# Opening of a spectral filter and maxout kernel: filter loads in three parts, PSUM tiles of two banks, another order of table columns

## The chip, the cores and the metric

The kernel runs on one core of one Trainium2 chip. The metric is the device time of one execution in microseconds (us). A core has TensorE (PE in the profile, with PEld for its weight loads), VectorE (DVE), ScalarE (ACT), GpSimd (POOL) and SyncE (SP), and 16 DMA engines that all queues share. The results of matmuls go to PSUM, which has eight banks of 2 KB on each of 128 partitions; VectorE and ScalarE empty them here, and GpSimd reads SBUF only. About 0.2% (1 us) is what a measurement of this kernel can tell from no change.

## The reference

The input x has 8 sequences of 3072 tokens of 256 channels. Each channel is filtered along the sequence in the frequency domain, and the result goes through a two-branch maxout layer:

```python
X = np.fft.rfft(x, axis=1)
Y = X * (filt_r + 1j * filt_i)[None]
y = np.fft.irfft(Y, n=3072, axis=1)            # 8 x 3072 x 256
g = np.maximum(y @ w1, y @ w2)                 # 24576 x 1024
out = g @ w_out                                # 24576 x 256
```

## The kernel before

**The transform as matmuls.** 3072 = 96 x 32. For a sequence, a first step multiplies by a cosine and sine table of size 96 (C1), a second one by a table of size 32 with the twiddle factors (U, one 64-column block for each of 24 values u), then comes the product with the filter, and the two steps go back (VP and VQ, then G1). A visit is a sixth of the frequencies; the index v (or n) counts six visits, each of two values w, and w, g gives u = 2w + g. The second step s2 (L371) leaves a pair of PSUM tiles px, s = 0 and 1, and the product of each with the filter (L380) gives a tile pq for the step back.

**The filter.** F (128 partitions) holds the filter in the order that px has. load_f (L109) fills partitions 0 to 31 and 64 to 95: 16 partitions with frequencies in rising order (L117), 16 with falling order (L120), and one more small load for the frequency at the fold (L124). These loads cast from float32 and go through GpSimd's queue. double_f (L128) copies each group of 32 partitions to the next 32, by VectorE (L130) or by SP's DMA (L132). The filter comes in two parts, WP: visits 0 to 3 (w 0 to 7), doubled by VectorE, and visits 4 and 5 (w 8 to 11), doubled by four DMAs on SP's queue. On that queue the four loads of the layer's weights (WS, L279) stand behind them.

**The opening, batch 0.** It is written out by hand from L562 on, and each engine runs its instructions in the order in which they are written. Tables are computed on VectorE and ScalarE (table_c, tables_u, sines_u). s1t (L495) does the first step for the eight tiles of x, each with two PSUM tiles pa, which ScalarE (for the last tiles VectorE too) writes to at2; spin (L556) fills TensorE with matmuls that compute nothing. t1 (L507) transposes at2 in six groups, one PSUM bank each, emptied by VectorE and ScalarE in turn to bt. table_v and put_v (L252, L267) make VP and VQ out of U, in two halves (h) and two kinds (q), with two banks and two or three evictions each; the factor one half of frequency zero is the scale hv in L272. s2 and the products of the six visits follow. For the visits in POOLED, ScalarE copies px of s = 1 to SBUF (stage_x, L591), and GpSimd multiplies it there; visit 5's is shared half and half by VectorE and GpSimd (L386). s3t (L518) does the step back of a visit into two PSUM banks pt, which ScalarE, and for visits 4 and 5 VectorE too, writes to zT. The visits go in the order 1, 0, 2, 3, 4, 5.

GpSimd's queue is, in order: eight loads of x, small tables, 18 filter loads, a load of x of batch 1, its products, two loads of x, half of Wd (L290), the load of Wo (L287), a load of x, the other half of Wd.

**The stream after it.** From L646 on, t2 brings zT to zr, s4 does the last step to y, and a loop over 64 token tiles does the layer: moe_h (L442; Wd = w1 - w2, a rectified product) and moe_o (L463), which adds y @ M, with M = w2 @ w_out. A list with planned steps places the work of the next batches in between: s1, visits (s2, products, s3, through DRAM with zd), z_read. The PSUM pools ps (six banks) and pso (two banks) serve the opening and the stream alike.

Of the kernel before, what the change touches and what calls it, by code (L numbers as in the profile page):

```python
# [11 lines left out]
OP = mybir.AluOpType  # L12
# [14 lines left out]
def kernel(  # L27
# [40 lines left out]
    ps = ctx.enter_context(tc.tile_pool(name="ps", bufs=6, space=bass.MemoryType.PSUM))  # L68
    pso = ctx.enter_context(tc.tile_pool(name="pso", bufs=2, space=bass.MemoryType.PSUM))
# [3 lines left out]
    pq0 = setup.enter_context(tc.tile_pool(name="pq0", bufs=6))  # L73
    ctx.enter_context(tc.manual_schedule())
# [33 lines left out]
    WP = ((0, 8), (8, 12))  # L108

    def load_f(h):  # L110
        w0, w1 = WP[h]
        n = 2 * (w1 - w0)
        for g in range(2):
            for ri, f in enumerate((filt_r, filt_i)):
                k0 = 24 * g + 2 * w0
                src = bass.AP(f.tensor, f.offset + k0 * D, [[96 * D, 16], [D, n], [1, D]])
                G.dma_start(out=F[64 * g:64 * g + 16, ri, w0:w1].rearrange("p w s d -> p (w s) d"), in_=src)  # L117
                n0 = 1 if k0 == 0 else 0
                src = bass.AP(f.tensor, f.offset + (96 - k0 - n0) * D, [[96 * D, 16], [-D, n - n0], [1, D]])
                G.dma_start(out=F[64 * g + 16:64 * g + 32, ri, w0:w1].rearrange("p w s d -> p (w s) d")[:, n0:n],  # L120
                            in_=src)
                if n0:
                    src = bass.AP(f.tensor, f.offset + 48 * D, [[96 * D, 16], [1, D]])
                    G.dma_start(out=F[16:32, ri, 0, 0], in_=src)  # L124
# [17 lines left out]

    V.memset(W1, 1.0)
# [3 lines left out]
    kc = init.tile([NP, NW, 2, 2], FP32)  # L147
    kap = init.tile([128, NW, 2], FP32)
# [3 lines left out]
    hv = init.tile([128, 2, 1], FP32)  # L152
    load_x(0, 0, 1)
    G.iota(pid, pattern=[[1, 1]], base=0, channel_multiplier=1, allow_small_or_imprecise_dtypes=True)
    G.iota(kc, pattern=[[2, NW], [24, 2], [1, 2]], base=0, channel_multiplier=0,
           allow_small_or_imprecise_dtypes=True)
    load_x(0, 1, 1)
    G.iota(kap, pattern=[[2, NW], [24, 2]], base=0, channel_multiplier=0,
# [4 lines left out]
    for c in range(3, 8):  # L163
        load_x(0, c, 1)
    for q in range(2):
        G.memset(hv[:, q], 1.0)
        for r in (0, 32):
            G.memset(hv[r:r + 1, q], 0.5 * (1 - q))
    load_f(0)
    load_f(1)  # L170
# [3 lines left out]
    def table_c():  # L174
# [4 lines left out]
        kf = kc.rearrange("p w g s -> p (w g s)")  # L179
# [16 lines left out]
    def tables_u():  # L196
# [24 lines left out]
        V.tensor_scalar(t1[:, 0], kap.rearrange("p w g -> p (w g)"), a_, base, OP.mult, OP.add)  # L221
# [19 lines left out]
    def sines_u(h):  # L241
        uv = ua.rearrange("p u c s j -> p u (c s j)")
        S.activation(U[:, NW * h:NW * h + NW], uv[:, NW * h:NW * h + NW], AF.Sin, bias=zero, scale=TWO_PI)

    def table_g():
        pg = ps.tile([96, NP], FP32, tag="ps", name="pg")
        TE.matmul(pg, C1, I128[0:NP, 0:NP], start=True, stop=True)
        S.activation(G1, pg, AF.Copy)

    def table_v(h, q):  # L250
        pool, tag = (pso, "po") if h else (ps, "ps")
        pv = [pool.tile([128, 6, 64], FP32, tag=tag, name="pv%d" % s) for s in range(2)]  # L252
        for i in range(6):
            for g in range(2):
                for s in range(2):
                    rows = slice(64 * s, 64 * s + 64)
                    u = 2 * (6 * h + i) + g
                    if q == 0:
                        TE.matmul(pv[s][64 * g:64 * g + 64, i], U[rows, u], I128[rows, rows], start=True, stop=True)
                    else:  # L260
                        TE.matmul(pv[s][64 * g:64 * g + 32, i], U[rows, u, 32:64], I128[rows, rows],
                                  start=True, stop=True)
                        TE.matmul(pv[s][64 * g + 32:64 * g + 64, i], U[rows, u, 0:32], NI[rows, rows],
# [3 lines left out]
    def put_v(h, q, pv):  # L267
        for s in range(2):
            i0 = 1 if h == 0 and s == 0 else 0
            tab = VQ if q else VP  # L270
            if i0:
                S.activation(tab[:, 0, 0], pv[0][:, 0], AF.Identity, bias=zero, scale=hv[:, q])  # L272
            S.activation(tab[:, 6 * h + i0:6 * h + 6, s], pv[s][:, i0:6], AF.Copy)  # L273
# [97 lines left out]
    def s2(b, v):  # L371
        px = [ps.tile([128, 2, D], FP32, tag="ps", name="px%d" % s) for s in range(2)]
        for i in range(2):
            for s, g in ((0, 0), (1, 1), (0, 1), (1, 0)):
                u = 2 * (2 * v + i) + g
# [4 lines left out]
    def product(E, v, s, px, pool=None):  # L380
# [3 lines left out]
        return pq  # L384

    def shared_product(v, s, px, xs_, pool):  # L386
        pq = pool.tile([128, 2, 2, D], BF16, tag="pq", name="pq")
        V.tensor_tensor(pq[:, 0], px, F[:, 0, 2 * v:2 * v + 2, s], OP.mult)
        G.tensor_tensor(pq[:, 1], xs_, F[:, 1, 2 * v:2 * v + 2, s], OP.mult)
        return pq  # L390

    def s3(b, v, pq):
# [9 lines left out]
        for g in range(2):  # L402
            S.activation(zt[:, :, g], pz[g], AF.Copy)  # L403
        nc.sync.dma_start(out=zd[b][4 * v:4 * v + 4].rearrange("u p d -> p u d"),
                          in_=zt.rearrange("p i g d -> p (i g) d"))
# [89 lines left out]
    def s1t(c):  # L495
        for dc in range(2):
            pa = ps.tile([128, 4, 96], FP32, tag="ps", name="pa")
            for m in range(4):
                TE.matmul(pa[:, m], xb[0, c][:, m, 128 * dc:128 * dc + 128], C1, start=True, stop=True)
            o_ = at2[:, dc].rearrange("p u q m -> p (u q) m")[:, :, 4 * c:4 * c + 4]  # L500
            i_ = pa.rearrange("p m q -> p q m")
            if dc == 1 and c >= 6:
                V.tensor_copy(o_, i_)
            else:
                S.activation(o_, i_, AF.Copy)

    def t1(n, engine):  # L507
        pb = ps.tile([128, 4, D], BF16, tag="ps", name="pb")
        for i in range(4):
            for dc in range(2):  # L510
                TE.transpose(pb[:, i, 128 * dc:128 * dc + 128],
                             at2[:, dc, 4 * n + i].rearrange("p q m -> p (q m)"), I128)
        if engine is S:
# [226 lines left out]
```

## Time and profile before

| | us |
|---|---|
| three runs | 503.47, 503.74, 504.51; median 503.74 |
| profiled execution | 503.8 |
| its span | 502.0 |
| TensorE busy | 488.4 (97%) |
| VectorE busy | 331.9 (66%) |
| ScalarE busy | 308.3 (61%) |
| GpSimd busy | 257.5 (51%) |

The profile is of one execution. Its views, which are quoted below, are: the page with the busy share of each engine in 40 slices of the span; windows, one line for each stretch, with the busy time of each engine in it and the count of its instructions, then the clock that was granted to TensorE (1.00 is full), the DMA engines' share and GB/s; the chain, which follows the work that ended last back from the end; and the instructions of an engine in order of time, each with its start, its length, the line of the kernel, the tile written and the tiles read, how many were merged into the row, and in brackets the idle time before it and what ended that. A DMA's row on a queue is the time of its issue; the time from issue to landing is given separately. L12 is line 12 of the kernel before.

### The profile page before, as it was taken

The numbers are of one execution on the slowest core, as the hardware profiler recorded it, in microseconds if no ns is written. First come the engines' busy times: TensorE is split into PE (matmuls) and PEld (weight loads), VectorE is DVE, ScalarE is ACT, GpSimd is POOL, SyncE is SP. The second block draws the span as 40 slices with busy tenths as digits, with TensorE's granted clock in tenths as the row PEclk, the third lists the DMA queues.
The fourth block names the chain that finished last, engine by engine and source line by source line (L and its number), as shares of the span: only waits on it lengthen the run. The fifth ranks groups of instructions, "written<-read, shape, count | busy, mean of one in ns | idle before, by whom it ended". The sixth has DMA issues, their size and how long they took to land.

```text
span 502.0 us, 13079 instructions
## 1 busy us (share of the span) xinstructions
PE 488.4 (97%) x5299; PEld 362.1 (72%) x5303; DVE 331.9 (66%) x518; ACT 308.3 (61%) x629; POOL 257.5 (51%) x338
## 2 busy tenths in 40 slices
PE   8688999999999999999999999999999999999997
PEld 3455777777777777777777777777777777777775
DVE  7876688457865777457765687557765687555553
ACT  6776478647774676557764586647774465544442
POOL 7893569547463864645654855537632221222220
PEclk9989999999999999999999999999999999999999
DMA  7999789995799667986779558896769235411112
GB/s 125 150 252 217 230 229 290 306 274 171 212 268 260 175 204 234 250 229 189 198 244 275 187 177 245 235 239 197 197 181 255 78 111 153 168 65 64 64 64 84
DMA packets 77966, 97.20 MB, mean 194 GB/s; under 512 B 8017, under 2 KB 54354, under 8 KB 77842
## 3 DMA queue, kind: packets, MB, share of 16 engines
q1 hardware_dynamic: 64642, 66.73, 49.6%
q0 software_dynamic: 13264, 29.64, 20.3%
q8 instruction: 41, 0.67, 0.6%
q14 instruction: 19, 0.16, 0.1%
HBM read 53.87 MB, written 47.19 MB: 201 GB/s over the span
## 4 chain that ended last, share of the span: by engine, by line
PE 90%; DMA 5%; POOL 2%; issue 1%; ACT 1%; DVE 0%; SPq 0%; POOLq 0%; DVEq 0%
PE po L476 34%; PE ph L448 33%; PE po L474 8%; PE pz L399 5%; PE py L428 4%; PE pa L349 2%; DMA F<-in_filt_r_dram 2%; PE px L376 2%; DMA Wo<-in_moe_w_out_dram 2%; POOL xb L88 1%; DMA F<-F 1%; PE pr L549 1%; POOL pq L382 0%; PE pt L528 0%; PE pm__1132 L306 0%
## 5 line engine op out<-in xcount | busy, mean ns | idle before, releaser
L476 PE MATMUL po<-Wo,gt 128*128 128x256 bf16 x1536 | 261.0, 273 | 0.2 <-DMA Wo<-in_moe_w_out_dram 0.2
L452 ACT ACTIVATE gt<-ph 128x384 bf16<-128x384 f32 x321 | 157.0, 496 | 147.9 <-PE ph L448 147.3
L461 POOL DMA_DIRECT2D out_dram<-ot x186 | 102.6, 555 | 187.1 <-DVE ot L488 184.4
L476 PEld LDWEIGHTS <-gt 128*128 128x128 bf16 x1536 | 146.6, 98 | 66.1 <-issue 10.3
L450 DVE TENSOR_SCALAR gt<-ph 128x384 bf16<-128x384 f32 x191 | 104.9, 552 | 63.1 <-PE ph L448 59.9
L382 DVE TENSOR_TENSOR pq<-px,F 128x1024 bf16<-128x1024 f32 x91 | 107.0, 1219 | 24.2 <-PE px L376 22.6
L448 PEld LDWEIGHTS <-Wd 128*128 128x128 bf16 x1024 | 96.5, 98 | 12.9 <-POOL Wd L292 1.4
L103 POOL TENSOR_TENSOR xb<-XF 128x512 bf16<-128x512 f32 x48 | 61.2, 1276 | 41.3 <-DMA XF<-in_x_dram 21.2
L488 DVE COPY ot<-po 128x512 f32<-128x512 f32 x95 | 65.1, 685 | 25.3 <-PE po L476 25.0
L104 POOL TENSOR_TENSOR xb<-XF 128x512 bf16<-128x512 f32 x48 | 61.0, 1271 | 0.0
L403 ACT ACTIVATE zt<-pz 128x512 bf16<-128x512 f32 x84 | 45.6, 595 | 11.5 <-PE pz L399 8.4
L353 ACT ACTIVATE at<-pa 128x512 bf16<-128x512 f32 x96 | 51.8, 610 | 1.2 <-PE pa L349 0.8
L428 PE MATMUL py<-G,zr 96*128 96x96 bf16 x512 | 32.7, 206 | 0.2
L428 PEld LDWEIGHTS <-zr 96*128 96x128 bf16 x512 | 29.0, 97 | 2.5 <-DVE zr L552 0.4
L399 PE MATMUL pz<-pq,VP 64*64 64x256 bf16 x336 | 21.9, 281 | 0.0
L376 PE MATMUL px<-bt,U 64*64 64x256 bf16 x384 | 19.8, 278 | 1.2 <-ACT VQ L273 0.7
L399 PE MATMUL pz<-pq,VQ 64*64 64x256 bf16 x336 | 20.9, 269 | 0.0
L349 PE MATMUL pa<-xb,CT 64*64 64x512 bf16 x192 | 19.5, 383 | 0.0
L399 PEld LDWEIGHTS <-VP 64*64 64x64 bf16 x336 | 9.7, 105 | 13.3 <-issue 13.3
L376 PEld LDWEIGHTS <-U 64*64 64x64 bf16 x384 | 10.4, 109 | 3.9 <-issue 3.3
L559 PE MATMUL pd<-W 128*128 128x512 bf16 x30 | 10.5, 462 | 1.7 <-DVE zero L145 1.5
L552 DVE COPY zr<-pr 96x1024 bf16<-96x1024 bf16 (+1 forms) x8 | 5.2, 649 | 8.0 <-PE pr L549 8.0
(429 smaller groups left out, 609.7 us busy)
## 6 DMA issues: line engine op xcount, KB each, us to landing
out_dram<-ot POOLq DMA_DIRECT2D x186, 128.0 KB, 3.3
XF<-in_x_dram SPq DMA_DIRECT2D x96, 192.0 KB, 4.6
ad<-at SPq DMA_DIRECT2D x56, 192.0 KB, 3.3
bt<-ad SPq DMA_DIRECT2D x14, 768.0 KB, 9.1
zd<-zt SPq DMA_DIRECT2D x42, 256.0 KB, 2.7
zr<-zd SPq DMA_DIRECT2D x56, 192.0 KB, 4.8
WS<-in_moe_w_dram SPq DMA_DIRECT2D x4, 512.0 KB, 5.1
xb<-in_x_dram POOLq DMA_DIRECT2D x8, 192.0 KB, 5.8
```

Source lines behind the costliest of these rows:

```text
L103: G.tensor_tensor(t_[:, 0], f[:, 0], f[:, 1], OP.add)
L104: G.tensor_tensor(t_[:, 1], f[:, 0], f[:, 1], OP.subtract)
L353: S.activation(at[:, m0:m0 + 2], pa[g], AF.Copy)
L382: E.tensor_tensor(pq, px.rearrange("p (o i) d -> p o i d", o=1).to_broadcast([128, 2, 2, D]), F[:, :, 2 * v:2 * v + 2, s], OP.mult)
L399: TE.matmul(pz[g][64 * s:64 * s + 64, i], tab[64 * g:64 * g + 64, 2 * v + i, s], pq[s][64 * g:64 * g + 64, q, i], start=(q == 0), stop=(q ...
L428: TE.matmul(py[:, m], zr[b][:, 4 * i + m, 128 * dc:128 * dc + 128], G1, start=True, stop=True)
L448: TE.matmul(ph, Wd[:, dc, 128 * j:128 * j + 128], y_[:, dc], start=(dc == 0), stop=(dc == 1))
L450: V.tensor_scalar(gt[tt][:, j], ph, 0.0, None, OP.max)
L452: S.activation(gt[tt][:, j], ph, AF.Relu)
L461: E.dma_start(out=dst, in_=ot[tt // 2][:, 3 * (tt % 2) + c])
L476: TE.matmul(p_, g_[:, n - 2, blk], Wo[:, n - 2], start=(e == 0), stop=(e == 9))
L488: V.tensor_copy(ot[tt // 2][:, e - 1:e + 1], po[0])
```

## The change

- **Filter in three parts.** WP is (0, 4), (4, 8), (8, 12). Only the first (visits 0 and 1) is doubled by VectorE; the second and third by SP's DMAs. The filter loads are 26.
- **Alternating partitions.** The rising and the falling frequencies stand on even and odd partitions of each group of 32, not on two blocks of 16. The columns of U, and so the rows of VP and VQ, follow: (c j s) for (c s j), and u = 4v + 2g + i for 2(2v + i) + g, also in the later batches.
- **Pairs of banks in the opening.** A pool named pair holds four tiles of two banks each, and every PSUM tile of the opening comes from it, the spin matmuls' too; ps and pso are made when it is given back. s1t, put_v and s3t empty a pair with one ScalarE instruction (s1t of the last tile and s3t of visit 5 with one of ScalarE and one of VectorE); t1 works on two groups at a time, one emptied by VectorE and one by ScalarE.
- **The factor one half** is put on a copy U0 of U's first block by one VectorE instruction, so put_v needs no eviction of its own for it.
- **Order of the opening.** sines_u(1) is written ahead of put_v; VectorE's doubling goes r before i; the visits go 0 to 5, with s3t right behind each visit's products for 0 to 3. POOLED is (2, 4, 5) for (0, 2, 3, 4), and visit 5 is no longer shared.

```diff
-    WP = ((0, 8), (8, 12))
+    WP = ((0, 4), (4, 8), (8, 12))
...
-                G.dma_start(out=F[64 * g:64 * g + 16, ri, w0:w1].rearrange("p w s d -> p (w s) d"), in_=src)
+                G.dma_start(out=F[64 * g:64 * g + 32:2, ri, w0:w1].rearrange("p w s d -> p (w s) d"), in_=src)
...
+    def two(name):
+        return pair.tile([128, 2, 512], FP32, tag="pair", name=name)
...
+    U0 = init.tile([128, 2, 64], BF16)
...
+    G.memset(hv, 1.0)
     for q in range(2):
-        G.memset(hv[:, q], 1.0)
-        for r in (0, 32):
-            G.memset(hv[r:r + 1, q], 0.5 * (1 - q))
-    load_f(0)
-    load_f(1)
+        G.memset(hv[0:64, q, 0:64:32], 0.5 * (1 - q))
+    for h in range(3):
+        load_f(h)
...
+        if h == 0:
+            V.tensor_tensor(U0, U[:, 0:1].to_broadcast([128, 2, 64]), hv, OP.mult)
...
     def put_v(h, q, pv):
-        for s in range(2):
-            i0 = 1 if h == 0 and s == 0 else 0
-            tab = VQ if q else VP
-            if i0:
-                S.activation(tab[:, 0, 0], pv[0][:, 0], AF.Identity, bias=zero, scale=hv[:, q])
-            S.activation(tab[:, 6 * h + i0:6 * h + 6, s], pv[s][:, i0:6], AF.Copy)
+        S.activation((VQ if q else VP)[:, 6 * h:6 * h + 6].rearrange("p i s m -> p s i m"), pv, AF.Copy)
...
     def s1t(c):
+        pa = two("pa")[:, :, 0:384].rearrange("p c (m q) -> p c m q", m=4)
...
+        if c < 7:
+            S.activation(o_, i_, AF.Copy)
         else:
-            V.tensor_copy(bt[0][:, 4 * n:4 * n + 4], pb)
+            S.activation(o_[:, 0], i_[:, 0], AF.Copy)
+            V.tensor_copy(o_[:, 1], i_[:, 1])
+
+    def t1(n):
+        pb = pair.tile([128, 2, 4, D], BF16, tag="pair", name="pb")
...
     def s3t(v, pq):
...
+        pz = two("pz").rearrange("p g (i s r c m) -> p g i s r c m", i=2, s=2, r=2, c=2)
...
+        if v < 5:
+            S.activation(zv, i_, AF.Copy)
+        else:
+            S.activation(zv[:, 0:2], i_[:, 0:2], AF.Copy)
+            V.tensor_copy(zv[:, 2:4], i_[:, 2:4])
...
-    for g in range(2):
-        for ri in range(2):
-            double_f(1, g, ri, nc.sync)
+    for h in (1, 2):
+        for g in range(2):
+            for ri in range(2):
+                double_f(h, g, ri, nc.sync)
...
-    for n in range(6):
-        t1(n, S if n % 2 else V)
-    put_v(0, 0, table_v(0, 0))
-    for g in range(2):
-        for ri in range(2):
+    for n in (0, 2, 4):
+        t1(n)
+    sines_u(1)
+    for ri in range(2):
+        for g in range(2):
             double_f(0, g, ri, V)
...
-    POOLED = (0, 2, 3, 4)
+    POOLED = (2, 4, 5)
...
-    pxs = {v: s2(0, v) for v in (1, 0)}
-    stage_x(0)
+    pxs = {v: s2(0, v) for v in (0, 1)}
+    put_v(0, 0, table_v(0, 0))
     put_v(0, 1, table_v(0, 1))
     pxs[2] = s2(0, 2)
     stage_x(2)
-    sines_u(1)
     put_v(1, 0, table_v(1, 0))
+    put_v(1, 1, table_v(1, 1))
     pxs[3] = s2(0, 3)
-    stage_x(3)
-    put_v(1, 1, table_v(1, 1))
-    for v in (1, 0, 2):
+    for v in range(4):
         pqs[v] = products(v)
-    s3t(1, pqs[1])
-    pxs[4] = s2(0, 4)
-    stage_x(4)
-    pqs[3] = products(3)
-    s3t(0, pqs[0])
-    pxs[5] = s2(0, 5)
-    stage_x(5)
-    for v in (2, 3):
         s3t(v, pqs[v])
+        if v < 2:
+            pxs[v + 4] = s2(0, v + 4)
+            stage_x(v + 4)
```

## The prediction

> **What bounds the kernel now.** I read the page first, then the stretches of the opening, then the chain that ended last, then each engine's instructions in order of time between 14 and 38 us.
>
> ```profile
> span 502.0 us, 13079 instructions
> PE   8688999999999999999999999999999999999997
> ```
>
> Each digit is 12.55 us. TensorE is full from the fifth digit on; only the first four have room, and every function whose work differs after the change and is not a mere renumbering runs there. Busy time of the engines (PE, PEld, DVE, ACT, POOL), granted clock, DMA share:
>
> ```profile
> 20.00:25.00 5.00, 2.47 (x111) 1.57 (x118) 4.47 (x5) 4.01 (x9) 4.93 (x5) 0.77 0.70 117
> 25.00:30.00 5.00, 4.53 (x128) 2.81 (x121) 4.57 (x5) 3.22 (x7) 5.00 (x3) 0.54 0.94 213
> 50.00:55.00 5.00, 5.00 (x44) 3.68 (x43) 3.86 (x8) 3.03 (x6) 0.00 (x0) 1.00 0.73 200
> ```
>
> From 50 us TensorE has no gap, so what the opening gains or loses goes to the end whole. The chain, in order of time (start, length):
>
> ```profile
> 16.69 4.13 DMA F<-in_filt_r_dram
> ...
> 21.61 3.23 DMA F<-F
> ...
> 30.64 2.10 POOL pq L382
> 32.73 1.15 POOL pq L389
> ...
> 37.19 9.41 DMA Wo<-in_moe_w_out_dram
> ```
>
> It runs over the filter's last part: load, copy into the second half of the partitions by SP's DMA, POOL's products of visits 4 and 5, then POOL's queue (two loads of x, Wd, Wo). Those engines one by one:
>
> ```profile
> 16.22 0.48 POOL L117 DMA_DIRECT2D F<-in_filt_r_dram  x1
> 16.69 0.54 POOL L120 DMA_DIRECT2D F<-in_filt_r_dram  x1
> ...
> 18.22 1.25 POOL L117 DMA_DIRECT2D F<-in_filt_r_dram  x1
> 19.57 1.49 POOL L120 DMA_DIRECT2D F<-in_filt_r_dram  x1
> 21.05 1.24 POOL L117 DMA_DIRECT2D F<-in_filt_i_dram  x1
> 22.28 1.17 POOL L120 DMA_DIRECT2D F<-in_filt_i_dram  x1
> ...
> 24.02 6.31 POOL L382 TENSOR_TENSOR pq<-xs,F 128x1024 bf16<-128x1024 f32 x3
> ```
> ```profile
> 18.15 1.22 DVE L130 COPY F<-F 32x4096 bf16<-32x4096 bf16 x1
> ...
> 19.72 3.60 DVE L130 COPY F<-F 32x4096 bf16<-32x4096 bf16 x3
> 23.82 5.75 DVE L382 TENSOR_TENSOR pq<-px,F 128x1024 bf16<-128x1024 f32 x5 [0.50 <-DVE F L130]
> 30.60 2.36 DVE L382 TENSOR_TENSOR pq<-px,F 128x1024 bf16<-128x1024 f32 x2 [1.03 <-DMA F<-F]
> ```
> ```profile
> 27.33 0.67 PE L376 MATMUL px<-bt,U 64*64 64x256 bf16 x8
> 27.44 1.09 ACT L538 ACTIVATE zT<-pt 128x512 bf16<-128x512 f32 x2 [1.07 <-PE pt L528]
> ```
>
> Three things are to be seen. A filter load costs POOL about 0.5 us to issue, 64 KB or 128 KB alike, but 1.17 to 1.49 us while VectorE's copies L130 run. VectorE then waits for SP's last copy until 30.60, and POOL takes up visit 4 at 30.63, so 30.5 is when the last copy landed. And TensorE computes the next px at 27.33 while ScalarE is only beginning to empty the pt before it: there is PSUM to spare.
>
> **The change, part by part.** The sum is made against the profiled execution, 503.8 us with a span of 502.0 (0.06 above the median of 503.74).
>
> *Loads of the filter, POOL's queue.* Eighteen loads become 26: eight more issues at 0.50 (start to start at 16.22, 16.69, 17.22, 17.69, 18.22) are +4.0 us. The ninth to sixteenth load of POOL's queue each starts just after a landing of the x load eight places earlier (9.92 after x3, 14.11 after x7, whose matmul starts at 13.88), so eight are in flight at most; that order stays. After the change the eighth filter load still goes at 14.11 and the other 18 follow. The ones after x7 start about 0.5 us earlier, since the 64 KB loads ahead land sooner (before, two waited until 14.88 and 15.66). VectorE's copies halve: 4 of 1.22 become 4 of about 0.65 (half, plus a little fixed cost). Four issues during the long copies took 5.15 us for 2.0, a loss of 3.1 in 4.9 us of copying; in proportion 2.6 us of copies cost 1.6, and if each issue just ends with the next copy, 0.4. I take 1.1, a relief of 2.0. Last issue: 22.28 + 4.0 - 0.5 - 2.0 = 23.8. Its landing took 4.1 with an issue of 1.17; with an issue of 0.53 it is 3.4, so 27.2 in place of 26.4. Bounds: 26.5 (no loss to copies) and 28.5.
> [...]
>
> *Copies on SP's queue.* Four of 128 KB become eight: visits 2 and 3 (part two) now come by DMA too. In the trace such a copy took 2.9, 3.2, 5.4 and 4.0 us from issue to landing. All are queued ahead of the four loads of WS, which move later with the last of them (27.01 before) by about 1; WS for Wd's first half landed at 32.7, over 2 us ahead of its use at 34.90. Last copy, with the last row's 4.0: 27.2 + 4.0 = 31.2 in place of 30.4. Bounds 29.4 (26.5 + 2.9) and 33.4 (28.0 + 5.4).
>
> *Products.* POOL's list (0, 2, 3, 4 and half of 5: 4 x 2.13 + 1.16 = 9.7 us) becomes (2, 4, 5): 6.4 us. But both 4 and 5 need the last copy, and behind it POOL now has 2 x 2.13 = 4.3 where it had 2.13 + 1.16. So POOL is through at 31.2 + 0.1 + 4.3 = 35.6 in place of 33.89: +1.7. VectorE does nine products instead of seven and a half, 10.9 for 9.2 us, but its copies are 2.3 shorter: it starts near 21.6, has done four by 26.3, waits for part two's copies (load issued about 20, landed 23.6, copied 27), and does 2 and 3 by 30.6 and the last two by 33.7. It is off the path.
>
> *PSUM pairs.* Eight banks are now four pairs. Program order alone says which pair each tile can get. While px0, px1 and px2 are alive, pv(1,0), pv(1,1) and px3 follow each other through one pair; px4 can only have pz0's pair, px5 only pz1's, after ScalarE has emptied them. These are new waits on TensorE's queue. What stands behind them there are the s3t matmuls, and behind those ScalarE's evictions. Durations: an eviction of 384 took 0.49, of 512 0.60; so 768 is 0.82 and 1024 is 1.0 (a 1024 row at 43.33 took 1.02), beside 0.87 and 1.09 for two single ones. Merging saves ScalarE about 0.05 each time. In order: t1 starts some 0.2 later (one eviction of 768 instead of two engines in x tile 6), ScalarE is through with bt at 19.1, the sines 0.93, 20.0; two put_v 21.65; xs2 22.25; put_v 23.1; then pv(1,1) on TensorE 0.75 with its hand-overs, put_v 24.7; px3 25.5; s3t(0) with its filler 1.6 at the granted clock of 0.54, 27.2; eviction 28.3; px4 29.0; s3t(1) 30.6; eviction 31.7; px5 32.3. From here 0.85 each on TensorE and 1.0 on ScalarE: evictions end at 34.3, 35.3 and 36.3, and the last half at 37.0, where the last one before ended at 35.07: +1.9. Bounds: +0.7, if TensorE is warm in s3t(0) and s3t(1) (0.9 for 1.6 twice), and +2.5.
>
> *Cheap or free.* The half-scale on U0 is one small VectorE instruction near 13, in a gap (VectorE waits 0.59 at 14.43). The six memsets of hv become three, 0.3 us ahead of the first load, given back at the wait on x3. The sines move from 22.40 to 19.1, taking away TensorE's 1.5 us wait for U; what is late next there is the pair of pv(1,1), costed above. The new order of rows in U, F, zt and the tables changes no size of any instruction from 50 us on: nothing, hidden or not.
>
> *Sum.* POOL's path +1.7 and ScalarE's +1.9 run side by side and meet in s3t(5) and Wd; the later sets it. Behind them the order is untouched: f1, t2, s4, the first moe_h need zT and Wd, and Wo is issued 3.3 us after POOL's products and landed 9.4 later, so all move by about 1.9. 503.8 + 1.9 = 505.7.
>
> **The rivals.**
> - *B, the last copy is slow.* The eight copies share the engines with x of batch 1 (384 KB, issued before at 23.43, landed at 28.7), as the third copy before did with 5.4 us. With the late bound T = 33.4 POOL ends at 37.8, +3.9: 507.7. For it: the DMA share of 0.94 at 25 to 30 us, and 0.5 MB more copies; against: only one copy of four took that long.
> - *C, no change.* Filter loads move at x's pace. x tiles of 192 KB came about 1.0 us apart, 190 KB per us; the first seven filter loads, 540 KB, landed from 13.9 to 17.6, 145 KB per us. On alternating partitions, with short latencies (26.5 + 2.9 = 29.4), POOL ends at 33.8, -0.1; a warm TensorE must then bring ScalarE's path to +0.7 or less: 503.7 to 504.5, I take 504.2. Against: in the second half the loads are spaced by their issue, not by their bytes. [...]
> - *D, faster.* POOL's 3.3 us of less work comes through, because POOL and not the filter was the limit: it ran from 24.02 to 30.33 without a break and met visit 4 at 30.63. Place: the last SP copy; it decides if that lands by 28.1, when POOL would leave v2 (26.0 + 2.1). POOL then ends at 32.4, -1.5: 502.3. Against: with the shortest latencies seen (3.4 and 2.9) the last load would have to be issued at 21.8, 17 issues in 7.1 us, 0.42 each, where the trace has 0.47 to 0.57.
>
> **How the numbers follow.** A, the forecast, 505.7: 0.55, own range +1.0 to +3.0. B 0.14, C 0.18, D 0.13. A measurement can tell about 0.2%, 1.0 us. D is faster, C the same, A and B slower, less 0.01 of A's low edge: 0.13, 0.19, 0.68. The range reaches over C and most of B, 502.9 to 508.0; D and B's upper edge, together under 0.2, lie outside.
>
> **What would show it.** Right: 26 filter loads, the last issued near 23.8; the last F<-F landing near 31; VectorE's products from about 21.6, with a wait for F<-F before visit 2; POOL idle before visit 4, its products ending near 35.6; TensorE waiting for zT evictions before px4 and px5 and for VQ before px3; Wo landing near 48.5 instead of 46.6; the stretches beyond 60 us unchanged. Wrong: POOL busy without a gap from its first product, or a last copy before 29, or px4 computed while pz0 is still full.

## The result and the profile after

The changed kernel takes 512.25 us (median of six runs, 511.18 to 513.96) against 503.75 (six runs, 503.42 to 504.51): a ratio of 1.017, with a 95% interval of 1.0149 to 1.0191. It is 8.5 us slower, where 1.9 were forecast; the range ended at 508.0. Its profiled execution took 512.8 us, the span is 511.0, 9.0 more than before.

The page of the changed kernel, the span and the slices (12.8 us each) of TensorE and of its clock:

```profile
span 511.0 us, 13076 instructions
PE   7677999999999999999999999999999999999996
PEclk9857999999999999999999999999999999999999
```

The loss is in the first four slices, as forecast: three of them hold less than before (8, 6, 8, 8 became 7, 6, 7, 7), and in the third the granted clock is 0.5. Stretches of the changed kernel (busy us of PE, PEld, DVE, ACT, POOL, then clock, DMA share, GB/s):

```profile
20.00:25.00 5.00, 2.35 (x139) 1.96 (x139) 4.76 (x7) 4.64 (x6) 5.00 (x10) 0.74 1.01 187
25.00:30.00 5.00, 3.55 (x89) 1.78 (x65) 5.00 (x5) 2.32 (x3) 2.44 (x2) 0.50 0.99 176
30.00:35.00 5.00, 3.89 (x84) 2.48 (x84) 1.28 (x2) 2.26 (x3) 0.00 (x0) 0.50 0.88 273
35.00:40.00 5.00, 2.56 (x81) 1.79 (x78) 2.36 (x2) 2.44 (x3) 4.45 (x3) 0.84 0.68 230
40.00:45.00 5.00, 3.59 (x42) 2.51 (x38) 1.11 (x2) 1.78 (x3) 4.97 (x6) 0.50 0.84 143
60.00:65.00 5.00, 5.00 (x48) 3.82 (x47) 3.89 (x7) 2.33 (x6) 1.35 (x3) 1.00 0.73 227
```

Three things differ from before. The DMA engines are full from 20 to 30 us (shares of 1.01 and 0.99, where they were 0.70 and 0.94). GpSimd does nothing at all between 30 and 35 us. And TensorE runs at half its clock for most of 25 to 45 us (0.50 granted in three of the four stretches, 0.84 in the other), where before it had 1.00 in every stretch from 30 us on.

The chain of the changed kernel that ended last, in order of time (start, length):

```profile
24.25 5.23 DMA F<-in_filt_i_dram
29.54 5.59 DMA F<-F
...
35.55 1.89 POOL pq L388
...
37.64 2.14 POOL pq L388
...
39.82 0.84 PE pz L526 x24
40.68 0.61 ACT zT L534
41.31 0.70 DVE zT L535
...
43.07 0.85 PE pr L546 x8
...
46.06 0.61 PE ph L448 x2
```

It is the chain of the forecast: the last load, the last copy, GpSimd's two products, the last s3t, then the step to the layer. GpSimd in order of time, changed kernel:

```profile
24.25 0.54 POOL L119 DMA_DIRECT2D F<-in_filt_i_dram  x1
24.78 0.52 POOL L87 DMA_DIRECT2D xb<-in_x_dram  x1
27.14 2.14 POOL L388 TENSOR_TENSOR pq<-xs,F 128x1024 bf16<-128x1024 f32 x1 [1.84 <-DMA F<-F]
35.55 4.21 POOL L388 TENSOR_TENSOR pq<-xs,F 128x1024 bf16<-128x1024 f32 x2 [6.28 <-ACT zT L532]
```

It stands idle for 6.28 us ahead of visit 4. The row names an eviction of ScalarE as what ended the wait, but what held it was the copy, which landed at 35.13: VectorE begins its last two products at 35.55 too, and in the kernel with single banks below both begin at 34.7, where the row names the copy. In both kernels the start comes 0.42 us after the landing (34.29 there). ScalarE's evictions of zT, changed kernel:

```profile
28.43 1.02 ACT L532 ACTIVATE zT<-pz 128x1024 bf16<-128x1024 f32 x1 [2.24 <-PE pz L526]
31.09 1.02 ACT L532 ACTIVATE zT<-pz 128x1024 bf16<-128x1024 f32 x1 [1.16 <-PE pz L526]
34.36 1.02 ACT L532 ACTIVATE zT<-pz 128x1024 bf16<-128x1024 f32 x1 [0.91 <-PE pz L526]
35.87 1.02 ACT L532 ACTIVATE zT<-pz 128x1024 bf16<-128x1024 f32 x1 [0.48 <-PE pz L526]
38.30 1.02 ACT L532 ACTIVATE zT<-pz 128x1024 bf16<-128x1024 f32 x1 [1.41 <-PE pz L526]
40.68 0.60 ACT L534 ACTIVATE zT<-pz 128x512 bf16<-128x512 f32 x1 [1.35 <-PE pz L526]
```

The moments side by side (us; "first ph" and "first po" are the first matmuls of the layer):

| | before | forecast | after |
|---|---|---|---|
| last filter load issued | 22.28 | 23.8 | 24.25 |
| landed | 26.4 | 27.2 | 29.48 |
| last copy F<-F landed | 30.5 | 31.2 | 35.13 |
| GpSimd's products through | 33.89 | 35.6 | 39.76 |
| zT complete | 35.19 | 37.0 | 42.0 |
| first ph | 37.48 | 39.4 | 46.06 |
| Wo landed | 46.6 | 48.5 | 50.8 |
| first po | 46.64 | 48.5 | 54.67 |

Of the 9.0 us, 5.9 are there when GpSimd is through, and 2.7 more come between that and the first ph.

### The profile page after: what moved, and what is told of

It is laid out like the page before. It is cut to its first block, busy times and chain, and to the rows that moved or that the text cites. A ratio compares the mean times of both kernels' runs of the same rounds, so it can differ in the third digit from the quotient of the medians.

```text
span 511.0 us, 13076 instructions
## 1 busy us (share of the span) xinstructions
PE 490.9 (96%) x5300; PEld 364.6 (71%) x5302; DVE 331.0 (65%) x518; ACT 307.7 (60%) x611; POOL 255.7 (50%) x341
## 4 chain that ended last, share of the span: by engine, by line
PE 82%; DMA 9%; POOL 4%; DVE 2%; issue 1%; ACT 1%; SPq 0%; POOLq 0%; ACTq 0%
PE po L476 31%; PE ph L448 29%; PE po L474 8%; PE pz L399 5%; PE py L428 4%; PE pa L351 2%; PE px L382 2%; DMA xb<-in_x_dram 2%; DMA zd<-zt 1%; DMA bt<-ad 1%; DMA XF<-in_x_dram 1%; DMA out_dram<-ot 1%; DMA F<-F 1%; DMA F<-in_filt_i_dram 1%; POOL F L116 1%
## 5 line engine op out<-in xcount | busy, mean ns | idle before, releaser
L388 DVE TENSOR_TENSOR pq<-px,F 128x1024 bf16<-128x1024 f32 x93 | 109.3, 1219 | 27.7 <-PE px L382 23.3
L382 PE MATMUL px<-bt,U 64*64 64x256 bf16 x384 | 19.7, 283 | 3.6 <-ACT VP L275 1.1
L382 PEld LDWEIGHTS <-U 64*64 64x64 bf16 x384 | 10.4, 109 | 6.2 <-issue 4.9
```

What stands on the lines that cost most here:

```text
L388: E.tensor_tensor(pq, px.rearrange("p (o i) d -> p o i d", o=1).to_broadcast([128, 2, 2, D]), F[:, :, 2 * v:2 * v + 2, s], OP.mult)
```

## The experiments

Ratios stand to the kernel before on the same chip, with 95% intervals. Where a diff starts from the changed kernel, it stands against 1.017.

### One part of the change alone, or undone

**Three parts alone** (the kernel before, with the filter's parts and the copies of the changed one):

```diff
-    WP = ((0, 8), (8, 12))
+    WP = ((0, 4), (4, 8), (8, 12))
...
-    load_f(0)
-    load_f(1)
+    for h in range(3):
+        load_f(h)
...
-    for g in range(2):
-        for ri in range(2):
-            double_f(1, g, ri, nc.sync)
+    for h in (1, 2):
+        for g in range(2):
+            for ri in range(2):
+                double_f(h, g, ri, nc.sync)
```

> The kernel before with the filter in three parts alone: 26 loads, eight F<-F copies on SP's queue, VectorE doubles only visits 0 and 1; blocks of 16 partitions, single banks, its own order and its own POOLED. Theory 'congestion': the last copy lands near 34 to 35 instead of 30.4, and of the two products behind it POOL has one and a half; the time rises by 3.5 to 5 on 504.3, to about 508.5. Theory 'pairs': the filter's parts cost nothing where the banks are single, the time stays within 1 of 504.3.

Measured: 509.38 us, ratio 1.0097 (1.0069 to 1.0126), 5.2 us more. Its chain:

```profile
25.12 3.19 DMA F<-in_filt_i_dram
28.36 6.00 DMA F<-F
35.12 2.13 POOL pq L382
...
43.14 0.59 PE ph L448 x2
```

The last copy takes 6.00 us and lands at 34.4, 3.9 later than before; GpSimd idles 2.60 us and is through at 38.36. So the three parts cost some 5 us with all of PSUM as it was. Of the 3.9 us, 2.8 are the later issue of the last load (25.12 for 22.28) and 2.0 the longer copy (6.00 for 4.03), while its landing is 0.9 shorter (3.19 for 4.11).

**Alternating partitions alone** (the kernel before):

```diff
-                G.dma_start(out=F[64 * g:64 * g + 16, ri, w0:w1]...
+                G.dma_start(out=F[64 * g:64 * g + 32:2, ri, w0:w1]...
...
-                G.dma_start(out=F[64 * g + 16:64 * g + 32, ri, w0:w1]...
+                G.dma_start(out=F[64 * g + 1:64 * g + 32:2, ri, w0:w1]...
...
-        S.activation(U[:, NW * h:NW * h + NW], uv[:, NW * h:NW * h + NW], AF.Sin, bias=zero, scale=TWO_PI)
+        us = slice(NW * h, NW * h + NW)
+        S.activation(U[:, us].rearrange("p u (c j s) -> p (u c) s j", c=2, s=2),
+                     uv[:, us].rearrange("p u (c s j) -> p (u c) s j", c=2, s=2), AF.Sin, bias=zero, scale=TWO_PI)
```

> The kernel before with the alternating partitions alone (F's rows, U's columns). Loads and copies keep their number and size. All theories but one expect no change, 503.8 to 504.8. [...]

Measured: 503.65 us (ten runs), ratio 0.9985 (0.9972 to 0.9997). At most a slight gain; no cost. The theory that the spread over partitions matters, which the next run's expectation states, is the one that looked for a change here. It is the fastest kernel of the study, by less than the 0.2% that were called the bound of a difference.

**Blocks of 16 partitions put back** (the changed kernel; the diff above the other way round).

> The changed kernel with the filter's signs and the columns of U back on two blocks of 16 partitions; all else as changed. Theory 'partitions' (the new spread over partitions slows the loads or the copies): the last F<-F copy lands at 32 or earlier instead of 35.1, and the time falls from 512.3 to about 508. Theory 'congestion' (too many copies and loads share the DMA engines between 20 and 35 us) and theory 'pairs' (waits for whole PSUM pairs) both expect no gain: 512 to 513, with loads that land a little later, since 16 neighbouring partitions take a load no faster.

Measured: 511.58 us, ratio 1.0137 (1.0114 to 1.016). Nearly all of the loss stays. Alternation is not its cause.

**Second part doubled by VectorE too** (the changed kernel, three parts, four copies on SP's queue):

```diff
-    for h in (1, 2):
-        for g in range(2):
-            for ri in range(2):
-                double_f(h, g, ri, nc.sync)
+    for g in range(2):
+        for ri in range(2):
+            double_f(2, g, ri, nc.sync)
...
+    for ri in range(2):
+        for g in range(2):
+            double_f(1, g, ri, V)
```

> The changed kernel with the second part of the filter doubled by VectorE too, so SP's queue has four F<-F copies instead of eight; loads, order and pairs stay. Theory 'congestion': without half a megabyte of copies the last load lands near 27.5 instead of 29.5 and the last copy near 31.5 instead of 35.1; POOL's products end near 36 instead of 39.8 and the time falls by 3 to 4, to about 508.5. Theory 'pairs': ScalarE's evictions and TensorE are held by each other and not by the copies, the time falls by 1 at most, to 511.3 or more.

Measured: 507.81 us, ratio 1.0075 (1.0054 to 1.0095). The 26 loads are all still there, and GpSimd in this kernel is through at 36.45, 3.3 earlier:

```profile
32.23 4.22 POOL L388 TENSOR_TENSOR pq<-xs,F 128x1024 bf16<-128x1024 f32 x2 [4.87 <-DMA F<-F]
```

So the four added copies are a cause: without them 3.5 us of loss stay out of 8.5. What the eight added loads cost by themselves is not shown. The ratio is that of two parts (next), but GpSimd waits for the last copy until 32.23 here, while there it takes up visit 4 at 30.43 with no wait for a copy of F. The pairs can hide this difference: in both kernels ScalarE evicts visits 2 to 4 without a gap, and zT is complete at 38.6.

**Two parts** (the changed kernel):

```diff
-    WP = ((0, 4), (4, 8), (8, 12))
+    WP = ((0, 8), (8, 12))
...
-    for h in range(3):
+    for h in range(2):
         load_f(h)
...
-    for h in (1, 2):
+    for h in (1,):
```

> The changed kernel with the filter in two parts as before: 18 loads, VectorE doubles visits 0 to 3, four F<-F copies; partitions, order and pairs as changed. Theory 'congestion': the last copy lands at 30.4 as in the kernel before, POOL's products end at 30.5 + 4.3 = 34.8, the time falls by about 5, to 507.3; what is left over 503.75 is POOL's longer tail and the pairs. Theory 'pairs': still 510 or more, since ScalarE empties the last pair near 40.

Measured: 507.88 us, ratio 1.0072 (1.0057 to 1.0087). With the parts undone 3.6 us of loss stay. The last filter load is issued at 20.20 and the last copy by 25.25; GpSimd, through at 35.51, now waits for ScalarE's copies of px (3.87 and 0.83 us, ahead of visits 4 and 5), not for the filter. ScalarE's evictions of visits 2 to 4, with the second part doubled by VectorE (above):

```profile
34.27 3.09 ACT L532 ACTIVATE zT<-pz 128x1024 bf16<-128x1024 f32 x3 [0.76 <-PE pz L526]
```

and with two parts:

```profile
34.05 3.09 ACT L532 ACTIVATE zT<-pz 128x1024 bf16<-128x1024 f32 x3 [0.75 <-PE pz L526]
```

That the pairs are the second cause is shown by the single banks below.

**Single banks** (the changed kernel, three parts; each tile of two banks becomes two tiles of one, and each merged eviction two):

```diff
-    pair = setup.enter_context(tc.tile_pool(name="pair", bufs=4, space=bass.MemoryType.PSUM))
+    pair = setup.enter_context(tc.tile_pool(name="pair", bufs=8, space=bass.MemoryType.PSUM))
...
-        return pair.tile([128, 2, 512], FP32, tag="pair", name=name)
+        return [pair.tile([128, 512], FP32, tag="pair", name="%s%d" % (name, k)) for k in range(2)]
...
-        S.activation((VQ if q else VP)[:, 6 * h:6 * h + 6].rearrange("p i s m -> p s i m"), pv, AF.Copy)
+        for s in range(2):
+            S.activation((VQ if q else VP)[:, 6 * h:6 * h + 6, s], pv[s], AF.Copy)
```

> The changed kernel with every PSUM tile of the opening in banks of its own (eight of one bank, two evictions for two banks), same order of work, same filter path. Theory 'pairs': without waits for whole pairs VectorE and ScalarE empty bt at the same time (bt done near 19 instead of 20.8), the last zT eviction is no longer behind ScalarE's (0.7), the time falls by 3 or more, to 509 or less. Theory 'congestion': POOL still ends its products near 39.5, since the last copy lands at 35; only the 0.7 at the end and some of the 1.4 us at the start of t1 come back where they count, and the time is 511 to 512.

Measured: 511.14 us, ratio 1.0135 (1.012 to 1.015): 6.8 us of the 8.5 stay. GpSimd in this kernel:

```profile
34.71 4.20 POOL L388 TENSOR_TENSOR pq<-xs,F 128x1024 bf16<-128x1024 f32 x2 [4.77 <-DMA F<-F]
```

The pairs are gone, ScalarE is done with bt at 18.93 instead of 20.84, and the fourth eviction of zT starts at 32.36 for 35.87; but everything then waits for the copy, only 0.8 us earlier than in the changed kernel. While the copy is late, the pairs are mostly hidden behind it.

**Two parts and single banks** (both diffs above on the changed kernel).

> The changed kernel with the filter in two parts and every PSUM tile of the opening in single banks. Two parts alone came to 507.9. Theory 'pairs': what is left comes from waits for whole pairs and from px4 and px5 behind evictions that now end bank by bank: VectorE's products start 0.7 to 0.9 earlier, zT is done near 37 instead of 38.6, the time is 506 to 506.5. If the order of the visits and POOLED are what is left (VectorE's nine products end near 34), it stays above 507.

Measured: 504.11 us (ten runs), ratio 1.0005 (0.9995 to 1.0015). The whole loss is gone. Alternation, U0, the order of visits and the new division of the products are still in this kernel and, taken together, cost nothing that can be measured. Three parts alone +5.2 and the pairs with two parts +3.6 make 8.8, near the 8.5 measured for both, but the two do not simply add up: beside three parts, single banks took off only 1.7 of the 8.5, and in single banks three parts leave 6.8.

### Why the last copy is late

**x of batch 1 out of the copies' way** (the changed kernel; the load is issued after GpSimd's products instead of after the last filter load):

```diff
     load_fn()
-    load_x(1, 0, 2)
...
-    for c in (2, 4):
+    for c in (0, 2, 4):
         load_x(1, c, 2)
```

> The changed kernel with the load of batch 1's first x tiles (384 KB as written, 768 KB read) issued behind POOL's products, not ahead of them. Theory 'congestion' in the form that any bytes count: F's last copies have the DMA engines more to themselves between 25 and 32 us, the last lands near 33.5 instead of 35.1, POOL is through 1.5 us earlier; f1(1, 0) then waits for this load (issued near 38, landed near 43), which is needed at 42; the time is 511 to 512.5. If only the number of loads and copies counts (each waits for the one before it), the last copy stays at 35 and the time rises, to 513.

Measured: 509.94 us, ratio 1.011 (1.0083 to 1.0138). Its chain:

```profile
23.91 3.71 DMA F<-in_filt_i_dram
27.67 2.78 DMA F<-F
30.87 3.00 POOL pq L387 x2
...
35.02 4.92 DMA xb<-in_x_dram
...
43.27 0.64 PE ph L447 x2
```

With eight copies and 26 loads as in the changed kernel, but without the 384 KB of x, the last load takes 3.71 us for 5.23 and the last copy 2.78 for 5.59: it lands at 30.45, 4.7 us earlier. What held the copies was the engines' time that this load took: the DMA share from 25 to 30 us is 0.74 without it, 0.99 with it. GpSimd's products end at 35.09. Only part of this reaches the end, since the first step of batch 1 now waits for its x, which lands at 39.9, and the first ph comes at 43.06.

**Three parts with x in the middle** (three parts alone; x of batch 1 behind GpSimd's third product):

```diff
-    load_x(1, 0, 2)
...
+    load_x(1, 0, 2)
     for v in (4, 5):
         pqs[v] = products(v)
```

> The kernel before with the filter in three parts, as in b1_threeparts, and with the load of batch 1's first x tiles (384 KB) issued by POOL behind its products of visits 0, 2 and 3 instead of ahead of them. In b1 that load was in flight together with the last F<-F copies, which took 6 us each, and the last landed at 34.4. Theory 'congestion by that load': the last copy takes 3 to 4 and lands by 31, POOL's products end near 34.5 instead of 38.4, zT near 36, and the time is 504.5 to 505.5 instead of 509.4. Rival 'too many copies': the eight copies hold each other, the last still lands near 34, the time stays above 508.

Measured: 511.08 us, ratio 1.0139 (1.012 to 1.0158), no faster than the three parts alone and rather slower. GpSimd is through at 35.9 for 38.36, so the copy is early again; but the load of x, issued at 32.07 beside the 2 MB of WS, takes 8.47 us, TensorE waits 3.5 us for it, and the first ph comes at 44.66 for 43.12. In each of these kernels something in the stretch took longer: the last copy in the changed one (5.59 us, 2.78 with x moved), x here (8.47, 5.35 before), the loads of WS in the next (a median of 8.7, 5.1 before).

**Single banks, x behind visit 2's product, and fillers** (the changed kernel, three parts; the single banks above, the fillers of the next experiment, and):

```diff
-    load_x(1, 0, 2)
...
         s3t(v, pqs[v])
+        if v == 2:
+            load_x(1, 0, 2)
```

> The changed kernel with three things undone or added at once: the load of batch 1's first x tiles issued by POOL behind its product of visit 2, single banks, and the fillers of e8_warm. If the three causes (that load's contention with the copies, waits for whole pairs, the cold clock) make up the loss, the last copy lands near 30.7, POOL's products end at 35.1, zT near 36.3 with a warm TensorE, and the time is 504.5 to 506. If something else of the change costs time, it stays above 507.

Measured: 509.16 us (507.23 to 510.87), ratio 1.01 (1.0064 to 1.0137), above the range that was expected. The last copy lands near 31.5 and GpSimd is through at 36.1, but it then waits 0.47 us for WS, which was pushed later and took 8.7 us, and the first ph comes at 40.13, 2.7 later than before. In none of the three places tried for x are the eight copies free.

### The low clock behind the last product

**Fillers in s3t** (the changed kernel; three to five matmuls that compute nothing, instead of one, at the head of the last four s3t):

```diff
-        TE.matmul(pz[:, 0].rearrange("p i s r c m -> p (i s r c m)"), W1[:, 0:128], W1, start=True, stop=True)
+        for _ in range({2: 3, 3: 3, 4: 4, 5: 5}.get(v, 1)):
+            TE.matmul(pz[:, 0].rearrange("p i s r c m -> p (i s r c m)"), W1[:, 0:128], W1, start=True, stop=True)
```

> The changed kernel with more filler matmuls ahead of s3t of visits 2 to 5 (3, 3, 4 and 5 instead of 1 each), which TensorE computes while it would wait for products; nothing else. Theory 'cold clock': with the granted clock at 1.00 from 38 us on instead of 0.50 between 40 and 45, the way from the last product (39.8) to the first ph (46.1) shrinks from 6.3 to about 4.4, and the time from 512.3 to about 510.5. If Wd and Wo hold the first matmuls of the layer anyway, no gain, 512 to 513; if the fillers stand in the way of s3t they cost up to 1.

Measured: 509.98 us, ratio 1.0118 (1.01 to 1.0135), 2.3 us less than the changed kernel. The stretches of this kernel:

```profile
40.00:50.00 10.00, 8.09 (x89) 4.92 (x83) 6.45 (x13) 5.89 (x12) 7.63 (x9) 1.00 0.97 144
...
30.00:40.00 10.00, 8.03 (x149) 4.04 (x147) 3.24 (x3) 4.69 (x5) 4.45 (x3) 0.74 0.77 247
```

and of the changed kernel:

```profile
40.00:50.00 10.00, 8.29 (x74) 5.36 (x71) 4.75 (x10) 4.57 (x9) 7.54 (x9) 0.69 0.99 149
...
30.00:40.00 10.00, 6.45 (x156) 4.28 (x158) 3.63 (x4) 4.69 (x5) 4.45 (x3) 0.67 0.78 252
```

GpSimd is through at the same 39.8 in both. With the fillers TensorE is busy for 8.03 us for 6.45 in the ten before 40 us, is granted a clock of 1.00 for 0.69 in the ten after it, and does the first ph at 44.33 for 46.06. So 1.7 of the 2.7 us between the last product and the first ph are the clock by these traces, and 2.3 by the times of the two kernels.

**The same fillers with two parts** (the two parts above).

> The changed kernel with the filter in two parts (507.88, 1.0072) and the fillers in s3t(2) to s3t(5) that took 2.3 us off the changed kernel (3, 3, 4, 5 for 1). With two parts the clock is 0.50 to 0.55 between 25 and 35 us and full from 35 us on. Theory 1 (the low clock costs only where the last evictions wait for s3t): clock full from about 32 us on, gain about 1 us, 506.9, ratio 1.005. Theory 2 (s3t is behind PSUM pairs, not behind its clock): no gain or a loss of up to 0.5 us by the fillers, 507.9 to 508.4, ratio 1.007 to 1.008.

Measured: 509.69 us, ratio 1.0107 (1.0087 to 1.0127), 1.8 us slower than without them. GpSimd is through at 35.77, as before them (35.51), zT is complete at 41.66 for 38.56. The clock did not rise with them (0.50 and 0.88 in the two halves of 30 to 40 us, 0.55 and 1.00 without), and the added matmuls stand on the path themselves.

**The same fillers with two parts and single banks.**

> Two parts and single banks (504.11, 1.0005), with the same fillers. It is the candidate to beat both kernels: the clock there is 0.50 at 25 to 30 us, 0.81 at 30 to 35. If TensorE sets the end of the opening, zT is done up to 0.5 us earlier and the time is 503.5, ratio 0.9995; if ScalarE's evictions and GpSimd's products set it, the fillers are hidden or cost up to 0.5 us, 504.1 to 504.6, ratio 1.0005 to 1.0015.

Measured: 505.49 us (eight runs), ratio 1.0029 (1.0019 to 1.0039), 1.4 us slower than without, though the clock between 30 and 35 us rose from 0.81 to 0.93: the same answer. The fillers were worth something only where the late copy made TensorE wait for products.

### What the pairs cost

**px4 and px5 ahead of the s3t** (the changed kernel with two parts):

```diff
-    for v in range(4):
-        pqs[v] = products(v)
+    pqs[0] = products(0)
+    pxs[4] = s2(0, 4)
+    stage_x(4)
+    pqs[1] = products(1)
+    s3t(0, pqs[0])
+    pqs[2] = products(2)
+    pxs[5] = s2(0, 5)
+    stage_x(5)
+    s3t(1, pqs[1])
+    pqs[3] = products(3)
+    for v in (2, 3):
         s3t(v, pqs[v])
-        if v < 2:
-            pxs[v + 4] = s2(0, v + 4)
-            stage_x(v + 4)
```

> The changed kernel with the filter in two parts, and with px4 computed ahead of s3t(0) and px5 ahead of s3t(1), so that px4 takes px0's pair as soon as VectorE is done with it, and px5 px2's; pairs and all evictions as changed. With two parts alone POOL waited 3.9 and 0.8 us for xs4 and xs5, which came behind the evictions of zT. Theory 'lock-step' (that wait is what is left of the loss): POOL's products end near 34 instead of 35.5, zT is done near 36.8 instead of 38.6 and the time falls from 507.9 to about 506. Rival: VectorE's nine products, the end of which at 34.7 sets s3t(5), hold it, and the time stays within 0.7 of 507.9.

Measured: 508.67 us, ratio 1.0075 (1.0051 to 1.01), no gain over 1.0072. px4 is computed at 27.33 for 29.07, but the filler of s3t(0) now starts at 29.59, where it started at 26.80, 1.62 us of it waiting for a product of VectorE. With four tiles the wait only moves.

**t1 in single banks** (the changed kernel with two parts; VectorE's and ScalarE's groups in a bank of their own pair each):

```diff
-        pb = pair.tile([128, 2, 4, D], BF16, tag="pair", name="pb")
+        pb = [pair.tile([128, 2, 4, D], BF16, tag="pair", name="pb%d" % k) for k in range(2)]
...
-                    TE.transpose(pb[:, k, i, 128 * dc:128 * dc + 128],
+                    TE.transpose(pb[k][:, 0, i, 128 * dc:128 * dc + 128],
...
-        V.tensor_copy(bt[0][:, 4 * n:4 * n + 4], pb[:, 0])
-        S.activation(bt[0][:, 4 * n + 4:4 * n + 8], pb[:, 1], AF.Copy)
+        V.tensor_copy(bt[0][:, 4 * n:4 * n + 4], pb[0][:, 0])
+        S.activation(bt[0][:, 4 * n + 4:4 * n + 8], pb[1][:, 0], AF.Copy)
```

> The changed kernel with the filter in two parts (507.88, 1.0072 of before), and t1 alone in single banks: its two groups, one emptied by VectorE and one by ScalarE, take one bank of two pair tiles each instead of the two halves of one. Question: how much of the pairs' 3.6 us is the whole-pair wait of bt. Theory 1 (the late bt counts): ScalarE is through with bt some 1 to 1.5 us earlier (19.9 with pairs), put_v and VP follow, the lock-step chain of px4, px5 and the evictions starts that much earlier: 506.5, ratio 1.0045. Theory 2 (the lock-step of px4 and px5 with the evictions of zT sets it, and VectorE's products, which wait for the filter, set its start): bt is earlier, the first products of VectorE stay where they are, 507.7, ratio 1.007.

Measured: 507.63 us, ratio 1.0065 (1.0042 to 1.0088), the same as 1.0072 within the intervals. ScalarE's first copy of bt starts 0.45 us after VectorE's instead of 0.72, and nothing behind it is earlier. The handing over in t1 is not what the pairs cost, as far as this kernel tells: each t1 takes two of the four pairs in it.

What they do cost is read from the two kernels with two parts, with pairs and with single banks. L520 is the filler that opens s3t, L382 is px. TensorE with pairs, in order of time (px3, the openings of s3t(0) and s3t(1) around px4):

```profile
25.18 0.64 PE L382 MATMUL px<-bt,U 64*64 64x256 bf16 x8 [0.94 <-ACT VQ L275]
26.80 0.59 PE L520 MATMUL pz<-W 128*128 128x512 bf16 x1 [0.98 <-DVE pq L388]
...
29.07 0.64 PE L382 MATMUL px<-bt,U 64*64 64x256 bf16 x8 [0.71 <-DVE pq L388]
30.20 0.59 PE L520 MATMUL pz<-W 128*128 128x512 bf16 x1 [0.49 <-DVE pq L388]
```

with single banks:

```profile
24.03 0.64 PE L382 MATMUL px<-bt,U 64*64 64x256 bf16 x7 [0.23 <-ACT VQ L276]
24.60 0.61 PE L520 MATMUL pz<-W 128*128 128x512 bf16 x1
...
26.97 1.01 PE L382 MATMUL px<-bt,U 64*64 64x256 bf16 x8
...
27.92 0.61 PE L520 MATMUL pz<-W 128*128 128x512 bf16 x1
```

Neither the filler nor px4 reads a product. With single banks they wait for nothing; with pairs the filler starts 0.1 us after VectorE's second product and px4 0.1 us after its fourth (1.14 each from 24.40), when both halves of the px pair of visit 0, and then of visit 1, have been read. Moments of the two kernels:

| | pairs | single banks | later by |
|---|---|---|---|
| VectorE's products start | 24.40 | 23.81 | 0.6 |
| eviction of zT, visit 0, starts | 28.40 | 27.07 | 1.3 |
| visit 1 | 31.79 | 29.53 | 2.3 |
| visit 2 | 34.05 | 31.61 | 2.4 |
| zT complete | 38.56 | 35.53 | 3.0 |
| first ph | 41.18 | 38.19 | 3.0 |

The steps are 0.6 us ahead of the products, 0.7 up to the eviction of visit 0, 1.0 more up to that of visit 1 (px4 and the next s3t wait 0.71 and 0.49), and 0.6 at the end, where VectorE empties its half of the last pair only after ScalarE has done with its own (37.87 after 37.24 and 0.60); with a bank each, both end at 35.4 and 35.5. By their ratios 3.4 us lie between the two kernels.

## Why the prediction was wrong

The sign, the place and both mechanisms were right. What failed first is the landing of the last copy: its two latencies, 3.4 us for the load and 4.0 for the copy, measured 5.23 and 5.59. The path through the pairs was also priced too low, and one term behind the products was missing.

- **Loads and GpSimd's queue: right.** 26 loads; the last is issued at 24.25 (23.8). Issues under VectorE's short copies took 0.63, 0.63, 0.75 and 0.70 us for 0.49 to 0.54 outside: a loss of 0.7, between the 0.4 and the 1.1 that the prediction named.
- **Landing of the last load: wrong, the first mis-sized term.** 3.4 us were taken, 5.23 measured. Loads issued between 13.5 and 20.1 us, when the first copy began, landed in 2.4 to 3.6 us; those issued from 20.6 on, beside the copies, in 4.0 to 5.3.
- **Last copy: wrong, the second mis-sized term.** 4.0 taken, 5.59 measured; the eight took 3.5, 5.4, 4.6, 4.4, 6.2, 5.5, 6.8 and 5.6, where the four of before took 2.9 to 5.4. The two terms and 0.45 of late issue put the last copy at 35.13 for 31.2, 3.9 us, and beyond the bound of 33.4. Against the kernel before it is 4.7 us later: 2.0 by the issue of the last load, 1.1 by its landing, 1.6 by the copy. The fault is in how they were priced: from the latencies of single rows in a stretch whose DMA share was 0.94 already, with 0.5 MB of copies added to it. The share went to 1.00 from 20 to 30 us, and the loads, the copies and x, all in flight together, became longer. That they share the engines is shown by taking the 384 KB of x away: 3.71 and 2.78 us with the same loads and copies.
- **GpSimd behind the last copy: right.** 4.2 us for 4.3, with GpSimd idle before visit 4. It starts 0.42 us after the landing, where 0.1 was taken; with four copies it was 0.16 (30.47 to 30.63 before).
- **The lock-step of the pairs: right in kind, wrong in one wait, too small in sum.** The evictions end at 29.45, 32.11, 35.38 and 36.89, forecast 28.3, 31.7, 34.3 and 35.3, so 0.4 to 1.6 later; the fifth and sixth are late because of GpSimd's products. px3 waits for VQ (0.91) and px5 for zT (1.11), as said. But px4 is computed at 28.32, without a wait, while pz0 is still full until 29.45: that was named as a sign of error, and it is one. px4 has the pair of px1, freed by a product of VectorE, as the kernel with two parts shows. Nor does program order alone tell who gets which pair: px5 starts right after the eviction of pz1 in the changed kernel (32.17), but at 31.68 in the kernel with two parts, before that eviction begins (31.79). The whole path was put at +1.9, beside the filter's; measured without the three parts it is +3.6. Not foreseen were VectorE and ScalarE emptying one pair one after the other, 0.6 us at the end, and bt: ScalarE is done with it at 20.84, not 19.1.
- **"All move by about 1.9" behind the products: wrong, the missing term.** From GpSimd's last product to the first ph it took 3.6 us before and 6.3 after. Some 2 of the 2.7 are the clock (1.7 by the traces with the fillers, 2.3 by the times), the rest was not taken apart; the handing over of the last pair is in it.
- **VectorE: off the path, as said, but later.** Its products start at 23.26, not 21.6, since bt is late, and so there is no wait before visit 2.
- **Wo: not the gate.** It landed at 50.8; the first po, at 54.67, came 3.9 us after it.
- **Beyond 60 us: nearly unchanged, right.** The first ph is 8.6 us later, the span 9.0; one new gap of 0.47 us stands near 71 us.
- **The rivals.** B named the mechanism, eight copies that share the engines with x, but took it for the less likely case and priced it at 3.9 us, since it moved all that follows by no more than the products: T of 33.4 came out as 35.13, and the 2.7 us behind the products were in no case. C's faster loads did not come from the partitions: between 13 and 40 us the 64 KB loads landed in a median of 3.3 us (real parts) and 3.1 (imaginary) with blocks (three parts alone), in 3.4 and 3.2 in the changed kernel. Its 145 KB per us was also too low: the seven loads hold 640 KB, not 540, which is 173. The alternation alone is worth 0.15% (at most 0.3% by its interval). D fell: GpSimd met the last copy far behind its earlier products, not ahead of it.
- **Slips in the working.** The upper bound of the last copy took 28.0 for the landing where the bound named was 28.5; 33.9 would still have been short of 35.13. The lower bound of ScalarE's path comes to +0.5 by its own terms, not +0.7. And of the loads said to start just after a landing, the first three start 2.7, 1.3 and 0.6 us after it. None of these decided the outcome.

What stays open: whether blocks put back for alternation, 1.0137 against 1.017 with intervals that overlap, differ at all; what the eight added loads cost without the added copies, in single banks; and how the 0.6 us ahead of the products in the pairs' kernel divide.

## What to carry to other kernels

A latency read in one trace was no price for the next: the last copy took 4.03 us as the last of four, 5.59 as the last of eight, 2.78 as the last of eight with x moved. Where the share is near full already (0.94 here), price an added copy by what it does to all that is in flight with it, and ask what large load stands in the same stretch; where that load was moved, TensorE waited 3.25 and 3.5 us for it. Tiles of two banks saved about 0.07 us for each merged eviction here (1.02 for 1.09) and halved the number of buffers, four for eight: find out which tile gets whose buffer, and which engines share one, before merging evictions. And a wait in front of TensorE can be paid twice, as here, where the clock in the 10 us behind it was 0.69, and 1.00 with the fillers.

## What the runs showed of the hardware

- The DMA engines were full (share 1.01 and 0.99) at only 187 and 176 GB/s by the profile's count, with casting loads of 64 KB, copies within SBUF of 128 KB and one load of x of 384 KB; the same trace moved 273 at a share of 0.88 between 30 and 35 us.
- One load of x of 384 KB took 5.3 us in the kernel before, 7.1 beside the eight copies, 8.47 beside the loads of WS.
- TensorE was granted half its clock while it was busy for 3.55 and 3.89 of 5 us (25 to 35 us of the changed kernel), and 0.54 of it while it was busy for 4.53 of 5 (25 to 30 us of the kernel before). With fillers that raised the busy time from 6.45 to 8.03 of 10 us, the clock of the next 10 us was 1.00 instead of 0.69.
- The first product behind the last copy began 0.42 us after its landing where eight copies were queued (changed kernel, and with x out of the way), 0.16 us where four were (before).
